# A new step table for the first stage, fixed for TensorE alone, with regrouped loads and plain v for four units

## The chip, the cores and the metric

The kernel runs on one core of a Trainium2 chip. The metric is device time in microseconds of one execution; the time before is 1538.48 us, the median of three runs (1537.49 to 1541.13).

## What is computed

Chunked attention over 8 batches, 8 heads, 576 positions and head size 64, in chunks of 64 positions, then two feed-forward layers on the 4608 tokens:

```python
scores = scale * np.matmul(q_c, k_c.transpose(0, 1, 2, 4, 3))
attn = np.exp(scores - max) ; attn = attn / (sum + 1e-09) ; x = np.matmul(attn, v_c)
x = (((x @ w1) * (x @ w2)) @ w3) @ w_out          # 512 -> 1024 -> 1024 -> 512
h = x @ w_in                                       # 512 -> 2048
out = (np.maximum(h, 0.0) + alpha * np.minimum(h, 0.0)) @ w_out2   # 2048 -> 512
```

The weights reach the kernel as 64-bit floats. It turns each into two 32-bit parts, a rounded high part (HI) and the rest (LO), and each product of the feed-forward layers is three TensorE passes over such parts.

## The kernel before

The tokens are nine blocks of 512 (`b`), each fed by two attention units of 256 tokens (`u = 2b, 2b + 1`). The whole program is written out at build time, and a scheduling layer adds all waits. It also chooses the order of each engine's instructions by a plan of its own, with the order in the code as priority; an instruction that is handed to `keep_in_program_order` keeps its place instead. In the kernel before, the switch `pinned` is off during the first stage, so all three compute engines are ordered by the plan there, and turned on for TensorE's matmuls and transposes after it.

The first stage is what this text is about. It does the attention of units 0 to 5, the first projections of blocks 0 to 2 (`LEAD`), the conversion of 40 weight halves, and the product of `w3` and `w_out` (the fold). Its steps stand in the string `STARTUP` (line 36), letter and number:

- An attention unit `n`: `S` scores (32 small matmuls on TensorE), `M` maximum (VectorE), `X` 16 exps (ScalarE), `Y` sum and division (VectorE), `T` 8 transposes (TensorE), `P` copy of these out of PSUM (ScalarE), `V` 32 small matmuls with v (TensorE), `c` copy of the HI part into `x` (ScalarE), `d` subtraction for the LO part (VectorE).
- A weight half `n`, of 40: `A` an Abs out of the loaded `raw` (ScalarE), `B` three operations (VectorE), `C` the HI cast (ScalarE), `D` two operations (VectorE), `E` two more (VectorE). Halves 0 to 15 are `w1` and `w2` (tiles `wa`), 16 to 23 `w_out` (`wo`), 24 to 39 `w3` (`w`). `raw` has three buffers, and step `A` issues the load of the half two further on; the `w3` halves share the three buffers of tag `gs`.
- A projection group: `a b.f` and `b b.f`, 12 matmuls of 512 columns each, with weight halves 2f and 2f + 1 (into banks `a` and `b`, or a pair `ab`, in turns); `k` copies the first out (ScalarE), `m` multiplies (VectorE) and writes the product to DRAM (`g_dram`).
- A fold: `h f.half`, 12 matmuls from `w3` half 24 + 2f + half and four `wo` halves; `s` and `w` split its sum into HI and LO (ScalarE, VectorE).

`lent` (line 396) says which PSUM pair a unit's scores take: units 0 and 2 `att`, 1 and 3 `p23`, all others `att`. A fold's sums lie in the two banks of `p23`, one pair for two values of f. All loads are issued by SP, one after the other (`load_unit`, line 214: q and k of a unit as two transfers, v as six, since half of v is written to the other half of the partitions, `1::2`, so that a unit's V goes round all four 64 x 64 quadrants of the array).

After the stage, `load_g` reads the products of blocks 0 to 2 back, `proj_wc` multiplies them by the folded weights (tiles `acc`), and units 6 and 7 are mixed in; then blocks 3 to 8 and the last layer follow, which the change leaves alone.

Of the kernel before, what the change touches and what calls it, by code (L numbers as in the profile page):

```python
# [34 lines left out]

STARTUP = """
    S0 M0 X0 A0 S1 Y0 M1 T0 P0 B0 X1 V0 D0 c0 Y1 C0 A1 d0 T1 A2 E0 P1 S2 B1 V1 A3 c1 M2 C1 d1 X2 D1 S3 B2 a0.0 M3 C2
    Y2 X3 E1 T2 D2 b0.0 B3 P2 Y3 k0.0 V2 C3 A4 m0.0 T3 c2 E2 P3 d2 a0.1 A5 D3 B4 V3 k0.1 E3 C4 c3 D4 b0.1 A6 d3 q4
    q5 E4 a1.0 m0.1 A7 B5 a0.2 k1.0 B6 C5 D5 C6 b1.0 D6 k0.2 E5 E6 A8 b0.2 m1.0 A9 B7 a1.1 m0.2 C7 D7 B8 a0.3 k1.1
    E7 C8 D8 A10 b1.1 k0.3 B9 E8 C9 b0.3 m1.1 A11 D9 B10 a1.2 m0.3 C10 E9 a0.4 k1.2 D10 A12 B11 b1.2 k0.4 E10 C11  # L40
    D11 A13 b0.4 m1.2 E11 B12 A14 a1.3 m0.4 C12 D12 a0.5 B13 k1.3 E12 C13 b1.3 D13 k0.5 A15 B14 E13 b0.5 C14 m1.3
    A16 D14 a1.4 m0.5 E14 B15 A17 a0.6 k1.4 B16 C15 D15 b1.4 C16 k0.6 D16 E15 b0.6 m1.4 A18 E16 B17 a1.5 A19 m0.6
    C17 D17 a0.7 k1.5 B18 E17 C18 b1.5 k0.7 D18 A20 B19 b0.7 m1.5 C19 E18 D19 A21 a1.6 m0.7 E19 S4 B20 k1.6 A22 b1.6
    M4 C20 D20 X4 B21 a1.7 m1.6 E20 b1.7 D21 k1.7 C21 Y4 A23 m1.7 T4 E21 P4 B22 A24 V4 B23 C22 c4 D22 C23 d4 E22 S5
    D23 A25 M5 E23 X5 B24 B25 D24 C24 C25 Y5 A26 E24 T5 P5 D25 h0.0 A27 B26 E25 C26 V5 D26 A28 h0.1 c5 B27 d5 C27 s0
    E26 a2.0 w0 A29 D27 h1.0 k2.0 B28 E27 C28 b2.0 D28 A30 B29 h1.1 m2.0 C29 E28 D29 A31 a2.1 s1 B30 w1 C30 E29 h2.0
    k2.1 D30 A32 B31 b2.1 E30 C31 D31 A33 h2.1 m2.1 E31 a2.2 s2 B32 A34 w2 C32 D32 h3.0 k2.2 B33 E32 C33 b2.2 D33
    A35 B34 h3.1 m2.2 C34 E33 D34 a2.3 A36 s3 B35 w3 C35 h4.0 E34 k2.3 D35 A37 b2.3 B36 E35 C36 h4.1 m2.3 A38 D36
    B37 a2.4 s4 E36 C37 w4 A39 h5.0 D37 k2.4 B38 E37 b2.4 C38 D38 B39 h5.1 m2.4 C39 E38 a2.5 s5 D39 w5 E39 h6.0 k2.5
    b2.5 h6.1 m2.5 a2.6 s6 w6 h7.0 k2.6 b2.6 h7.1 m2.6 a2.7 s7 w7 b2.7 k2.7 m2.7  # L50
# [8 lines left out]
def tile_attention_moe_moe(ctx: ExitStack, tc: tile.TileContext, qkv: bass.AP, w12: bass.AP,  # L59
# [30 lines left out]
    pinned = [False]  # L90

    def matmul(*args, **kw):
        ins = nc.tensor.matmul(*args, **kw)  # L93
        if pinned[0]:
            tc.keep_in_program_order(ins)

    def transpose(*args, **kw):
        ins = nc.tensor.transpose(*args, **kw)  # L98
        if pinned[0]:
            tc.keep_in_program_order(ins)  # L100

    def split(dst, src):

        nc.scalar.copy(dst[:, HI], src)  # L104
        nc.vector.tensor_tensor(out=dst[:, LO], in0=src, in1=dst[:, HI].bitcast(F32), op=ALU.subtract)  # L105
# [51 lines left out]
    def convert_b(i):
# [3 lines left out]
        nc.vector.tensor_scalar(out=m, in0=m, scalar1=EXP_MIN, scalar2=EXP_MAX, op0=ALU.max, op1=ALU.min)  # L161
        nc.vector.tensor_scalar(out=m.bitcast(U32), in0=m.bitcast(U32), scalar1=3, scalar2=0x3FFFFFF8,
                                op0=ALU.logical_shift_left, op1=ALU.bitwise_and)
        nc.vector.scalar_tensor_tensor(out=m.bitcast(U32), in0=conv_raw[i][:, :, 1], scalar=0xC0000000,  # L164
                                       in1=m.bitcast(U32), op0=ALU.bitwise_and, op1=ALU.bitwise_or)

    def convert_c(i):
        nc.scalar.copy(w_g[conv[i]][:, HI], conv_m[i])

    def convert_d(i):  # L170

        p = conv_p[i] = tmp("p")
# [31 lines left out]
    def mm3(ps, stat, mov, first, last):  # L204
        for i, (s, m) in enumerate(PASSES):
            matmul(ps, stat(s), mov(m), start=first and i == 0, stop=last and i == 2)
# [3 lines left out]

    x_t = {}
    un = {}

    def load_unit(u):
# [4 lines left out]
        else:  # L219
# [3 lines left out]
                 "e": granule(slots[3], "e", F32).rearrange("p j (a h k) -> p j a h k", a=4, h=2)}  # L223
        v = un[u]["v"]
# [342 lines left out]
```

## Time and profile before

| | us |
|---|---|
| median of three runs | 1538.48 |
| profiled execution | 1539.19 |
| its span | 1537.4 |
| TensorE busy in the span | 1494.1 (97%) |
| VectorE busy | 780.4 (51%) |
| ScalarE busy | 422.6 (27%) |
| share of TensorE in the chain that ended last | 89% |

The profile is of one execution. Its time is the span, from the first to the last instruction, and 1.8 us around it. Busy shares are means over stages: in the last four fifths of the span TensorE is busy 9 tenths or more of every slice, so what can be read for the first stage has to be read from its own stretch, here 0 to 245 us.

### The profile page before, as it was taken

To read this page: it belongs to the slowest core of one execution; us is meant where nothing else is said; L and a number is where in the kernel's file an instruction comes from. 1 tells how busy PE (TensorE), PEld (TensorE's weight loads), DVE (VectorE), ACT (ScalarE), POOL (GpSimd) and SP (SyncE) were. 2 spreads that over 40 slices of the span, in tenths; PEclk is the share of its full clock that TensorE was granted. 3 is DMA by queue.
4 is the path that set the end of the run, shared out by engine and by line. 5 is a ranking of instruction groups with operands and counts; after the bars stand their busy time and mean duration, and the time that the engine had idled before them with its cause. 6 is when DMAs were issued, how large, how long until landed. Compare 5 with 4: busy or idle time off the path is not lost.

```text
span 1537.4 us, 21112 instructions
## 1 busy us (share of the span) xinstructions
PE 1494.1 (97%) x8688; PEld 1231.1 (80%) x8688; DVE 780.4 (51%) x1250; ACT 422.6 (27%) x1107; POOL 0.7 (0%) x6
## 2 busy tenths in 40 slices
PE   4997999999999999999999999999999999999998
PEld 3785787788888888888888888888888888888887
DVE  4989963366667665331334344343434344343433
ACT  6535323444444443331211111111111111111111
POOL 0000000000000000000000000000000000000000
PEclk9998999999999999999999999999999999999999
DMA  8644425644545456236501000010101000000000
GB/s 249 190 165 151 136 98 165 192 153 155 188 163 192 151 179 206 83 103 199 165 0 55 1 20 36 1 55 0 56 0 38 18 7 35 1 28 0 28 1 28
DMA packets 65041, 141.89 MB, mean 92 GB/s; under 512 B 6833, under 2 KB 25265, under 8 KB 64945
## 3 DMA queue, kind: packets, MB, share of 16 engines
q1 hardware_dynamic: 64944, 140.54, 27.7%
q8 instruction: 68, 1.11, 0.3%
q14 instruction: 29, 0.23, 0.0%
HBM read 98.57 MB, written 41.94 MB: 91 GB/s over the span
## 4 chain that ended last, share of the span: by engine, by line
PE 89%; DVE 4%; DMA 3%; ACT 2%; SPq 1%; issue 1%; ACTq 0%; DVEq 0%
PE acc L93 38%; PE a L93 23%; PE b L93 22%; PE wc L93 2%; PE ab L93 2%; DMA v<-in_qkv 1%; ACT e L258 1%; PE sc L93 1%; PE pa L93 1%; DMA raw<-in_wo 1%; DMA raw<-in_w 1%; PE pa L98 1%; DVE p L175 1%; DMA g<-g_dram 1%; DVE m L164 0%
## 5 line engine op out<-in xcount | busy, mean ns | idle before, releaser
L93 PE MATMUL acc<-w,gs 128*128 128x512 f32 x1728 | 414.7, 389 | 0.0
L93 PEld LDWEIGHTS acc<-w,gs 128*128 128x128 f32 x1728 | 324.4, 188 | 67.2
L104 ACT CAST gs<-g 128x512 fp32r<-128x512 f32 x168 | 104.6, 622 | 660.7 <-DVE g L378 635.0
L93 PE MATMUL acc<-gs,wc 128*128 128x512 f32 x864 | 210.2, 395 | 3.8 <-DVE gs L105 3.8
L93 PE MATMUL a<-y,w 128*128 128x512 f32 x864 | 207.5, 389 | 0.0
L93 PE MATMUL b<-y,w 128*128 128x512 f32 x864 | 207.5, 389 | 0.0
L93 PEld LDWEIGHTS acc<-gs,wc 128*128 128x128 f32 x864 | 161.6, 189 | 40.4 <-DVE gs L105 5.5
L93 PEld LDWEIGHTS b<-y,w 128*128 128x128 f32 x864 | 162.2, 188 | 33.7
L93 PEld LDWEIGHTS a<-y,w 128*128 128x128 f32 x864 | 162.2, 188 | 33.7
L105 DVE TENSOR_TENSOR gs<-g,gs 128x512 fp32r<-128x512 f32 x168 | 116.2, 692 | 134.7 <-ACT gs L104 132.7
L93 PE MATMUL a<-x,wa 128*128 128x512 f32 x720 | 175.1, 393 | 2.4 <-DVE x L297 2.4
L93 PE MATMUL b<-x,wa 128*128 128x512 f32 x720 | 175.7, 393 | 0.0
L93 PEld LDWEIGHTS a<-x,wa 128*128 128x128 f32 x720 | 136.3, 190 | 31.3 <-DVE x L297 2.9
L93 PEld LDWEIGHTS b<-x,wa 128*128 128x128 f32 x720 | 133.5, 188 | 27.6
L377 DVE TENSOR_SCALAR g<-b,alpha_sb 128x512 f32<-128x512 f32 x72 | 54.0, 750 | 177.7 <-PE b L93 177.7
L377 DVE TENSOR_SCALAR g<-a,alpha_sb 128x512 f32<-128x512 f32 x72 | 54.0, 750 | 162.6 <-PE a L93 162.6
L258 ACT ACTIVATE e<-sc,mx 128x64 f32<-128x64 f32 x288 | 85.7, 348 | 31.4 <-DVE mx L247 31.4
L331 DVE TENSOR_TENSOR a<-b,a 128x512 f32<-128x512 f32 x60 | 41.3, 688 | 95.1 <-PE b L93 84.4
L258 ACT ACTIVATION_READ_ACCUMULATOR e<-sc,mx 128x1 f32 x288 | 69.7, 242 | 0.0
L93 PE MATMUL ab<-x,wa 128*128 128x512 f32 x288 | 69.3, 390 | 0.0
L486 ACT COPY a<-a 128x512 f32<-128x512 f32 x48 | 28.6, 596 | 131.2 <-PE a L93 112.5
L93 PEld LDWEIGHTS ab<-x,wa 128*128 128x128 f32 x288 | 53.9, 188 | 11.2
(56 smaller groups left out, 995.9 us busy)
## 6 DMA issues: line engine op xcount, KB each, us to landing
qk<-in_qkv SPq DMA_DIRECT2D x36, 512.0 KB, 4.9
raw<-in_w2nd SPq DMA_DIRECT2D x32, 512.0 KB, 4.0
w_dram<-wm SPq DMA_DIRECT2D x32, 512.0 KB, 3.3
w<-w_dram SPq DMA_DIRECT2D x32, 512.0 KB, 3.3
y_dram<-y SPq DMA_DIRECT2D x36, 256.0 KB, 2.9
yraw<-y_dram SPq DMA_DIRECT2D x18, 512.0 KB, 4.3
out<-o SPq DMA_DIRECT2D x36, 256.0 KB, 2.1
raw<-in_w SPq DMA_DIRECT2D x16, 512.0 KB, 4.2
```

The costliest lines, as they stand in the source:

```text
L93: ins = nc.tensor.matmul(*args, **kw)
L98: ins = nc.tensor.transpose(*args, **kw)
L104: nc.scalar.copy(dst[:, HI], src)
L105: nc.vector.tensor_tensor(out=dst[:, LO], in0=src, in1=dst[:, HI].bitcast(F32), op=ALU.subtract)
L175: nc.vector.scalar_tensor_tensor(out=p, in0=conv_raw[i][:, :, 0], scalar=2.0 ** -52, in1=p, op0=ALU.mult, op1=ALU.mult)
L258: nc.scalar.activation(out=e[:, j, a, h], in_=s[:, h2, n * D:(n + 1) * D], func=AF.Exp, bias=mx[:, h2, n:n + 1], scale=SCALE, accum_out=sm ...
L331: nc.vector.tensor_tensor(out=a, in0=ps, in1=a, op=ALU.mult)
L377: nc.vector.tensor_scalar(out=g, in0=ps, scalar1=0.0, scalar2=alpha_sb[:, f:f + 1], op0=ALU.min, op1=ALU.mult)
L486: nc.scalar.copy(a, pa)
```

## The change

The table `STARTUP` is new. Its order is now fixed for TensorE from the first instruction on, while ScalarE and VectorE still follow the plan, with the table as priority. `InOrder` wraps the three engines; its switch is on for TensorE alone. Units 4 and 5 stand earlier in the table, the folds stand later and in runs, and the last two steps, `g`, load the first two products back before the last fold's split. Here is one line of the old table and one of the new, of the stretch where units 4 and 5 stand:

```diff
-    M4 C20 D20 X4 B21 a1.7 m1.6 E20 b1.7 D21 k1.7 C21 Y4 A23 m1.7 T4 E21 P4 B22 A24 V4 B23 C22 c4 D22 C23 d4 E22 S5
+    b1.0 m0.3 k1.0 B9 A10 D9 C9 a0.4 m1.0 E9 A11 M4 b0.4 k0.4 B11 X4 D11 a1.1 m0.4 B10 b1.1 D10 C11 A12 E11 C10 k1.1
...
+    class InOrder:
+        def __init__(self, engine):
+            self.engine, self.on = engine, engine is nc.tensor
+        def __getattr__(self, name):
+            op = getattr(self.engine, name)
+            def call(*args, **kw):
+                ins = op(*args, **kw)
+                if self.on:
+                    tc.keep_in_program_order(ins)
+            return call
+    pe, act, dve = InOrder(nc.tensor), InOrder(nc.scalar), InOrder(nc.vector)
...
+    CROSS = 4
...
+    def load_v(u):
         v = un[u]["v"]
         for j in range(2):
-            nc.sync.dma_start(out=un[u]["qk"][j], in_=qkv[2 * u + j, :, 0:2])
-        for j in range(2):
+            if u < CROSS:
+                nc.sync.dma_start(out=v[:, j].rearrange("p a x -> p (a x)"), in_=qkv[2 * u + j, :, 2])
+                continue
...
-                            a, h = 2 * i + odd, h2 ^ odd
+                            a, h = 2 * i + odd, h2 ^ (odd if u >= CROSS else 0)
...
-            if f % 2 == 0:
-                ab["fold"] = pair("p23", "wc")
-        ps = ab["fold"][:, f % 2]
+            ab["fold", f] = pair(("att", "p23")[f % 2], "wc")[:, 0]
+        ps = ab["fold", f]
...
+    act.activation(out=work.tile([P, 1], F32, tag="warm", name="warm", bufs=1), in_=ident[:, 0:1], func=AF.Exp)
     for u in range(4):
-        load_unit(u)
-        if u < RAW:
-            convert_load(u)
+        unit_tiles(u)
+    for load, n in ((load_qk, 0), (convert_load, 0), (load_qk, 1), (load_v, 0), (convert_load, 1), (load_v, 1),
+                    (load_qk, 2), (convert_load, 2), (load_v, 2), (load_qk, 3), (load_v, 3)):
+        load(n)
     nc.sync.dma_start(out=alpha_sb, in_=alpha)
-    lent = {0: "att", 1: "p23", 2: "att", 3: "p23"}
+    steps = [(b, f) for b in range(LEAD) for f in range(NF1)]
+    lent = {1: "p23", 3: "p23", 5: "p23"}
...
+        elif kind == "g":
+            load_g(*steps[n])
...
-    pinned[0] = True
+    act.on = dve.on = False
     load_unit(2 * LEAD)
-    load_g(*steps[0])
-    load_g(*steps[1])
```

So for units 0 to 3 v is loaded as two plain transfers a unit instead of six, and their V alternates between two quadrants of the array; the exps of these units write their results in the plain order too. A one-column exp stands ahead of everything on ScalarE. Unit 5 uses the pair `p23`, and each fold takes one bank of `att` or of `p23` by turns.

SP issues the loads at the start of the program in this order before, here the first ones:

```order
L226 DMA qk<-in_qkv 128x1024 x2
L229 DMA v<-in_qkv 128x2x128
L230 DMA v<-in_qkv 64x2x128
L231 DMA v<-in_qkv 64x2x128
L229 DMA v<-in_qkv 128x2x128
L230 DMA v<-in_qkv 64x2x128
L231 DMA v<-in_qkv 64x2x128
L143 DMA raw<-in_w 128x1024
L226 DMA qk<-in_qkv 128x1024 x2
```

and in this order now:

```order
L238 DMA qk<-in_qkv 128x1024 x2
L148 DMA raw<-in_w 128x1024
L238 DMA qk<-in_qkv 128x1024 x2
L244 DMA v<-in_qkv 128x512 x2
L148 DMA raw<-in_w 128x1024
L244 DMA v<-in_qkv 128x512 x2
L238 DMA qk<-in_qkv 128x1024 x2
L148 DMA raw<-in_w 128x1024
```

The second pair of `qk` (unit 1) stands in the fourth place instead of the tenth, and v of a unit is one row of two.

TensorE's first instructions before, up to the first projection groups (`sc` scores, `pa<-ident,e` transposes, `pa<-pt,v` values, `a`, `b` and `ab` projections):

```order
L93 MATMUL sc<-qk 64x64 x64
L98 MATMUL pa<-ident,e 128x128 x8
L93 MATMUL pa<-pt,v 64x64 x32
L98 MATMUL pa<-ident,e 128x128 x8
L93 MATMUL sc<-qk 64x64 x32
L93 MATMUL pa<-pt,v 64x64 x32
L93 MATMUL sc<-qk 64x64 x32
L93 MATMUL a<-x,wa 128x512 x12
L93 MATMUL b<-x,wa 128x512 x6
```

and now:

```order
L100 MATMUL sc<-qk 64x64 x64
L100 MATMUL pa<-ident,e 128x128 x8
L100 MATMUL pa<-pt,v 64x64 x32
L100 MATMUL pa<-ident,e 128x128 x8
L100 MATMUL pa<-pt,v 64x64 x32
L100 MATMUL sc<-qk 64x64 x32
L100 MATMUL a<-x,wa 128x512 x12
L100 MATMUL b<-x,wa 128x512 x12
L100 MATMUL ab<-x,wa 128x512 x12
L100 MATMUL sc<-qk 64x64 x32
L100 MATMUL pa<-ident,e 128x128 x8
```

The scores of unit 3 moved from ahead of the first group to behind the third, and those of unit 2 behind the values of unit 1.

TensorE again, where the folds (`wc`) begin, before:

```order
L93 MATMUL ab<-x,wa 128x512 x24
L98 MATMUL pa<-ident,e 128x128 x8
L93 MATMUL pa<-pt,v 64x64 x32
L93 MATMUL sc<-qk 64x64 x32
L93 MATMUL wc<-wo,w_1485 128x512 x12
L98 MATMUL pa<-ident,e 128x128 x8
L93 MATMUL wc<-wo,w_1571 128x512 x4
L93 MATMUL pa<-pt,v 64x64 x32
L93 MATMUL wc<-wo,w_1571 128x512 x8
L93 MATMUL a<-x,wa 128x512 x12
L93 MATMUL wc<-wo,w_1612 128x512 x12
L93 MATMUL b<-x,wa 128x512 x12
```

and now:

```order
L100 MATMUL ab<-x,wa 128x512 x24
L100 MATMUL wc<-wo,w_1657 128x512 x12
L100 MATMUL wc<-wo,w_1686 128x512 x12
L100 MATMUL wc<-wo,w_1752 128x512 x12
L100 MATMUL wc<-wo,w_1795 128x512 x12
L100 MATMUL a<-x,wa 128x512 x12
L100 MATMUL b<-x,wa 128x512 x12
L100 MATMUL wc<-wo,w_1815 128x512 x12
L100 MATMUL wc<-wo,w_1826 128x512 x12
L100 MATMUL wc<-wo,w_1868 128x512 x12
```

The steps of units 4 and 5 are gone from this place (they stand among the groups of blocks 0 and 1), and the folds stand in runs of three to five where every one had a projection group behind it.

## Rows read from the trace of the kernel before

**Rows 1.** The page, chain that ended last: share by engine.

```profile
PE 89%; DVE 4%; DMA 3%; ACT 2%; SPq 1%; issue 1%; ACTq 0%; DVEq 0%
```

**Rows 2.** Stretches: length; busy (instructions) by engine; PE clock; DMA share, GB/s.

```profile
core 0: us, PE busy (x) PEld busy (x) DVE busy (x) ACT busy (x) POOL busy (x), PEclk, DMA share, GB/s
0.00:20.00 20.00, 6.91 (x152) 5.78 (x156) 6.57 (x12) 8.17 (x39) 0.70 (x6) 1.00 0.91 277
20.00:40.00 20.00, 11.23 (x266) 10.01 (x259) 13.79 (x26) 15.38 (x71) 0.00 (x0) 0.86 0.74 223
...
60.00:80.00 20.00, 20.00 (x90) 16.57 (x89) 18.94 (x38) 7.20 (x12) 0.00 (x0) 1.00 0.52 164
...
120.00:140.00 20.00, 16.35 (x191) 13.11 (x189) 18.75 (x37) 12.28 (x44) 0.00 (x0) 1.00 0.48 160
140.00:160.00 20.00, 12.71 (x160) 9.39 (x160) 19.46 (x39) 12.37 (x44) 0.00 (x0) 0.66 0.37 120
```

**Rows 3.** TensorE's timeline, 16 to 67: start, busy us, what, [idle before, releaser].

```profile
16.53 1.94 PE L98 MATMUL pa<-ident,e 128*128 128x128 f32 x8 [0.89 <-DVE e L265]
19.57 1.99 PE L93 MATMUL pa<-pt,v 64*64 64x64 f32 x64 [1.10 <-ACT pt L276]
...
35.65 1.99 PE L93 MATMUL sc<-qk 64*64 64x64 f32 x64 [4.18 <-DVE x L297]
37.57 4.74 PE L93 MATMUL a<-x,wa 128*128 128x512 f32 x12
...
47.68 1.16 PE L93 MATMUL pa<-pt,v 64*64 64x64 f32 x64
...
61.93 2.88 PE L93 MATMUL b<-x,wa 128*128 128x512 f32 x12
64.65 2.88 PE L93 MATMUL ab<-x,wa 128*128 128x512 f32 x12
```

**Rows 4.** Timeline of ScalarE and VectorE, 8 to 27.

```profile
8.50 1.28 ACT L258 ACT_TABLE_LOAD   x1 [8.50 <-DVE mx L247]
9.79 0.31 ACT L258 ACTIVATE e<-sc,mx 128x64 f32<-128x64 f32 x1
...
14.43 0.75 ACT L155 ACTIVATE m<-raw 128x512 f32<-128x512 f32 x1
...
18.50 1.01 ACT L276 COPY pt<-pa 128x1024 f32<-128x1024 f32 x1 [3.32 <-PE pa L98]
...
24.04 1.11 ACT L300 CAST x<-pa 128x1024 fp32r<-128x1024 f32 x1
...
24.93 0.74 ACT L168 CAST wa<-m 128x512 fp32r<-128x512 f32 x1
...
25.92 1.22 DVE L297 TENSOR_TENSOR x<-pa,x 128x1024 fp32r<-128x1024 f32 x1
```

**Rows 5.** Transfers, 0 to 40: bytes moved, in 40 slices of 1 us.

```profile
GB/s 0 57 246 377 391 324 171 166 266 303 401 396 332 225 255 272 262 418 387 291 229 277 271 311 397 379 306 157 104 229 295 336 422 234 0 0 16 0 258 242
```

**Rows 6.** TensorE's timeline around units 4 and 5, and at the stage's end.

```profile
135.95 1.06 PE L98 MATMUL pa<-ident,e 128*128 128x128 f32 x8 [1.82 <-DVE e L265]
...
142.54 1.98 PE L93 MATMUL sc<-qk 64*64 64x64 f32 x64 [3.21 <-DVE x L297]
...
149.97 4.39 PE L93 MATMUL wc<-wo,w 128*128 128x512 f32 x10 [3.02 <-DVE w L180]
...
161.01 3.02 PE L93 MATMUL a<-x,wa 128*128 128x512 f32 x12 [1.41 <-DVE x L297]
...
245.30 4.60 PE L93 MATMUL acc<-gs,wc 128*128 128x512 f32 x12 [2.39 <-DVE gs L105]
```

**Rows 7.** VectorE's timeline in its dense stretch; the last row ends conversion 7.

```profile
68.94 0.68 DVE L179 TENSOR_TENSOR m<-m,wa 128x512 f32<-128x512 f32 x1
69.54 0.42 DVE L161 TENSOR_SCALAR m<-m 128x512 f32<-128x512 f32 x1
69.88 0.69 DVE L180 TENSOR_TENSOR wa<-m,p 128x512 fp32r<-128x512 f32 x1
```

**Rows 8.** The timeline where conversion 39, the last of the stage, ends.

```profile
222.68 0.69 DVE L180 TENSOR_TENSOR w<-m,p 128x512 fp32r<-128x512 f32 x1
```

More of the change, by code (lines that the diff above doesn't have):

```diff
@@ L36 @@
 STARTUP = """
[L37 to L41, printed above, removed]
@@ L88, in tile_attention_moe_moe @@
     w2_dram = {(f, h): tc.dram_tile([P, 2, TB], F32, name=f"w2_dram{f}_{h}") for f in range(NF2) for h in range(2)}
[L90 to L100, printed above, removed]
+    class InOrder:
[9 more added lines that the diff above has]
+    pe, act, dve = InOrder(nc.tensor), InOrder(nc.scalar), InOrder(nc.vector)
     def split(dst, src):
-        nc.scalar.copy(dst[:, HI], src)
-        nc.vector.tensor_tensor(out=dst[:, LO], in0=src, in1=dst[:, HI].bitcast(F32), op=ALU.subtract)
+        act.copy(dst[:, HI], src)
+        dve.tensor_tensor(out=dst[:, LO], in0=src, in1=dst[:, HI].bitcast(F32), op=ALU.subtract)
     def tmp(name):
@@ L205, in mm3, with unit_tiles @@
         for i, (s, m) in enumerate(PASSES):
-            matmul(ps, stat(s), mov(m), start=first and i == 0, stop=last and i == 2)
+            pe.matmul(ps, stat(s), mov(m), start=first and i == 0, stop=last and i == 2)
+    CROSS = 4
     x_t = {}
     un = {}
-    def load_unit(u):
+    def unit_tiles(u):
         if u < 4:
@@ L223, in load_unit, with load_qk @@
                  "e": granule(slots[3], "e", F32).rearrange("p j (a h k) -> p j a h k", a=4, h=2)}
+    def load_unit(u):
+        unit_tiles(u)
+        load_qk(u)
+        load_v(u)
+    def load_qk(u):
+        for j in range(2):
+            nc.sync.dma_start(out=un[u]["qk"][j], in_=qkv[2 * u + j, :, 0:2])
+    def load_v(u):
         v = un[u]["v"]
         for j in range(2):
-            nc.sync.dma_start(out=un[u]["qk"][j], in_=qkv[2 * u + j, :, 0:2])
-        for j in range(2):
+            if u < CROSS:
+                nc.sync.dma_start(out=v[:, j].rearrange("p a x -> p (a x)"), in_=qkv[2 * u + j, :, 2])
+                continue
             vs = qkv[2 * u + j, :, 2].rearrange("p (a x) -> p a x", a=4)
@@ L296, in attn_out @@
         if lo:
-            nc.vector.tensor_tensor(out=xs[LO], in0=pa, in1=xs[HI].bitcast(F32), op=ALU.subtract)
+            dve.tensor_tensor(out=xs[LO], in0=pa, in1=xs[HI].bitcast(F32), op=ALU.subtract)
             un.pop(u)
         else:
-            nc.scalar.copy(xs[HI], pa)
+            act.copy(xs[HI], pa)
     wc_g = {}
@@ L318, in fold_split @@
             wc_g[f] = granule(24 + f, "wc")
-        dst, ps = wc_g[f], ab["fold"][:, f % 2]
+        dst, ps = wc_g[f], ab["fold", f]
         if lo:
-            nc.vector.tensor_tensor(out=dst[:, LO], in0=ps, in1=dst[:, HI].bitcast(F32), op=ALU.subtract)
+            dve.tensor_tensor(out=dst[:, LO], in0=ps, in1=dst[:, HI].bitcast(F32), op=ALU.subtract)
         else:
-            nc.scalar.copy(dst[:, HI], ps)
+            act.copy(dst[:, HI], ps)
     def proj1(b, f, which, ps):
@@ L330, in product @@
     def product(b, f, a, ps):
-        nc.vector.tensor_tensor(out=a, in0=ps, in1=a, op=ALU.mult)
+        dve.tensor_tensor(out=a, in0=ps, in1=a, op=ALU.mult)
         if b < LEAD:
@@ L376, in proj2 @@
         g = tmp("g2")
-        nc.vector.tensor_scalar(out=g, in0=ps, scalar1=0.0, scalar2=alpha_sb[:, f:f + 1], op0=ALU.min, op1=ALU.mult)
-        nc.vector.scalar_tensor_tensor(out=g, in0=ps, scalar=0.0, in1=g, op0=ALU.max, op1=ALU.add)
+        dve.tensor_scalar(out=g, in0=ps, scalar1=0.0, scalar2=alpha_sb[:, f:f + 1], op0=ALU.min, op1=ALU.mult)
+        dve.scalar_tensor_tensor(out=g, in0=ps, scalar=0.0, in1=g, op0=ALU.max, op1=ALU.add)
         split_g(b, (f, 2), g)
@@ L420, in tile_attention_moe_moe @@
             a = ab[tuple(rest)][2] = tmp("a")
-            nc.scalar.copy(a, ab[tuple(rest)][0])
+            act.copy(a, ab[tuple(rest)][0])
         elif kind == "b":
@@ L456, in unit_steps @@
         return [first, second, third, fourth]
-    pinned[0] = True
+    act.on = dve.on = False
     load_unit(2 * LEAD)
-    steps = [(b, f) for b in range(LEAD) for f in range(NF1)]
-    load_g(*steps[0])
-    load_g(*steps[1])
     todo = {}
@@ L485, in tile_attention_moe_moe @@
             a = tmp("a")
-            nc.scalar.copy(a, pa)
+            act.copy(a, pa)
             if parts and f % 4 == 0:
```

64 lines of the change are left out of this document (35 added, 29 removed).

## The prediction

> **What bounds the kernel now.** I read the page's chain first: TensorE carries 89% of it [rows 1], so time is won only where TensorE waits or runs slowly. The table of 20 us stretches says where that is [rows 2]: it is busy 6.91 and 11.23 us in the first two, full at 60 to 80, then 16.35 and 12.71 at 120 to 160, the last at a granted clock of 0.66 (1.0 is 2.4 GHz). All of that lies in the first stage, before the first acc matmul at 245.30. TensorE's timeline gives its parts [rows 3, 6]: the first full group of 12 matmuls starts at 37.57, groups follow at 2.72 us (61.93, 64.65), and from 37.57 to 245.30 there are 207.7 us. In them lie 64 groups (174.1), two S, four T and four V of the attention units (1.16, 1.06 and 1.16 each, 11.2) and 1.9 for the first group, run cold (4.74 against 2.88). The remaining 20.5 us are waits and half clock. The named waits are 1.82, 3.21, 3.02 and 1.41 around units 4 and 5, and 2.39 for the first g [rows 6]. VectorE sets the pace of what can be brought forward: 18.94 of 20 us busy at 60 to 80, 19.46 at 140 to 160 [rows 2].
>
> I write S, T, V for a unit's scores, transposes and values on TensorE, X for its exps, P and c for its two ScalarE copies, d for VectorE's subtraction, as the table of steps does.
>
> **The loads and unit 0 and 1: the start moves from 37.57 to 29.5.** Before, q and k of unit 1 are issued behind six v pieces and a weight half, some 3.0 MB with themselves; now they are 2.5 MB. The rate by single us is 377 and 391 GB/s while q and k of unit 0 move and 171 and 166 just after, when the v pieces are under way [rows 5]. The first four slices hold 1.07 MB, the other 1.4 take 4 to 5 us at 277 to 390 GB/s, so unit 1's scores can end at 11 to 12; before, they stood ahead of the transposes at 16.53 [rows 3]. X0 loses the table load of 1.28 at its head [rows 4], since the one-column exp loads the table while nothing is ready: 8.5 + 16 exps from 9.79 to 14.43 (4.64) gives 13.1. Then comes the Abs of the second weight half (0.75), which needs its load, 3.5 MB into the queue; then X1, to 18.5 (before, it ends where c0 starts, 24.04). On ScalarE stand behind it a weight cast (0.7) and P0 (1.01): 20.2. The rest is a chain of cold steps: V0 1.99, T1 1.94, P1 1.01, V1 1.99, c1 1.11, d1 1.22 [rows 3, 4], 9.3 us, so 29.5. S2 (1.99) lies beside c1 and d1. I take 29.5. Bounds: 26 (clock up from T1 on, loads never late) to 34 (X1 waits for its weight half until 17).
>
> *What the pages say of the loads.* The Trainium skill, DMA: Bandwidth & Descriptors, Specifications, puts line rate at pieces of 512 B and more; the v pieces have 512 B, so by it plain v saves issue time only. This trace does not agree: 166 to 171 GB/s against 377 to 391. By the page's rule the mean rate of 277 GB/s [rows 2] would stay, the second weight half would land near 14 and the start be about 30.5.
>
> **V of units 0 to 3, uncrossed.** The same 32 matmuls now alternate between two quadrants of the array where they went round four. The trace has only four-quadrant V: 1.16 us, 1.99 cold [rows 3]. The price is between a little below nothing and a doubling, 2 x 1.99 + 2 x 1.16 = 6.3 us in all. I take nothing: S visits its quadrants in another sequence and takes the same 1.99, which looks like a limit per matmul and not per quadrant.
>
> **The order on TensorE.** Units 4 and 5 now come among the groups of blocks 0 and 1, with groups between S, T and V; before, each of their steps waited for its neighbour. That takes away the 9.5 us of waits named above and the half clock around them. The first two g loads, their casts and subtractions move ahead of the last split (and on SP ahead of unit 6's loads), so the 2.39 goes, and the first acc group, cold at 4.60, should take 2.88: another 1.7. The last fold's split (ScalarE, VectorE) ends some 1.4 us after the last fold, while acc matmuls of the other bank pair run: 0.4 left. Unit 6 loads into slots that the last folds read, so its load now starts two groups before acc; two groups and the twelve acc matmuls, about 7.6 us, hide it, and what lands later is a wait at its scores.
>
> New waits. TensorE can't change its order any more, so it stands where a weight is late. VectorE's order has, up to and with the last operation of conversion 7 (needed by b0.3), 46 us of work at 0.60 for a two-operand instruction, 0.34 for TENSOR_SCALAR and 1.22 for 1024 columns [rows 4, 7]; before, it was 48 and done at 70.6, so 22 us were idle. If the idle time shrinks with the start by some 8, conversion 7 is done at 62. TensorE would like it at 29.5 + 1.9 + 7 x 2.72 + six unit steps (6.9) = 57. The loads of units 4 and 5, 3 MB in 16 issues, now stand on SP's queue between weight halves 5 and 9; at 277 GB/s they take 11 us, of which I count what these halves come late among the waits. So **5 us** of waits, bounds 0 to 9. After that TensorE has 56 groups and five unit steps, 158 us, and the last fold starts at 62 + 2.7 + 155 = 220; VectorE has 134 us of work to conversion 39. Before, 130 us of it took from 70.6 to 223.4 [rows 7, 8], 1.17 us for each; at that pace 39 is done at 62 + 157 = 219, just in time, and part of that pace was waiting for folds. But folds now run three to five in a row with only three w3 buffers, where before every fold had a projection group behind it. I take **3 us**, bounds 0 to 10.
>
> **The sum.** First acc at 29.5 + 174.1 + three S, four T, four V (12.4) + 1.9 + 5 + 3 + 0.4 = 226.3, against 245.30: 19.0. With 1.7 for the warm first acc group, 20.7 us. The rest of the kernel keeps its order. The profiled execution took 1539.2 (span 1537.4), 0.7 above the median; 1539.2 - 20.7 = 1518.5, and I say **1519**.
>
> **Rivals.** (1) *Conversions no earlier.* The early idle time of VectorE stays 22 us, because loads and ScalarE set it; conversion 7 at 70.6, 8.6 later: 1527. For: VectorE has little idle time left at 60 to 80 [rows 2]. Against: its idle 13 us of the first 20 [rows 2] come from the load order that changes. (2) *The loads bring nothing*, the first group starts at 37 since the engines that move data are the bound: 7.5 later, 1526. That is the case in which the change does not do what it says. For: data moves at 277 GB/s in the first 20 us [rows 2]. Against: 377 and 391 stand beside it where no v pieces move [rows 5]. (3) *V doubles*, two quadrants instead of four: +6.3, 1525. The mechanism is that matmuls of one quadrant follow each other without overlap; against it stands S. The Trainium skill, TensorEngine Tiling (Array Packing), Tiling Modes, has four independent tiles at 64 x 64, which would speak for it; no run here shows two. (4) *Slower: the runs of folds starve.* A w3 half is cast into a buffer that frees with the fold three before; the cast stands in ScalarE's queue, and behind it the next Abs and the copy that frees a projection bank. From the fourth fold on, 13 folds: if each exposes its cast (0.7), its two last VectorE operations (1.3) and a share of another conversion's, 2.8 us, that is 36 in place of my 3: 1552. It decides from 1.8 us a fold. Against: before, VectorE waited for such casts, but TensorE's timeline has no wait between the 1.41 at 161 and the 2.39 at 245 [rows 6], because groups lay between; now runs of 8 to 13 us are followed by 5 to 11 us of projections, in which the buffers refill.
>
> **How the numbers follow.** My case 57%; rival 1 14%, rival 3 10%, rival 2 8%, rival 4 7%, and 4% that losses of several kinds add up to no change. A measurement here tells 0.2% (3 us) from none. Faster: 57 + 14 + 10 + 8 = 89%; same 4%; slower 7%. My own case goes from 1509 (start at 27, no new waits from late weights) to 1528; rivals 1 to 3 lie at 1525 to 1527 with a few us of spread. The range 1509 to 1531 leaves out rival 4, the unchanged case and the ends of the rest, some 19%.
>
> **What would show it.** Right: first group of 12 at 27 to 32; X1 beginning within a us of X0's end; no TensorE wait over 1 us between 75 and 200; clock 1.00 at 140 to 160; first acc at 222 to 230 with a first group under 3 us. Wrong: the first group at 35 or later (loads); VectorE idle over 18 us before conversion 7 (rival 1); V at 2 us warm (rival 3); waits for w from VectorE or ScalarE before most folds (rival 4); long waits of unit 6's scores for q and k.

## The result: 15 us slower, since every 512-column matmul became slower

The changed kernel takes 1554.29 us (median of four runs, 1554.05 to 1554.65) against 1538.85 for the kernel before beside it: ratio 1.0099, 95% interval 1.0082 to 1.0117. The forecast was 1519, range 1509 to 1531. Spans of the profiled executions: 1552.4 after, 1537.4 before.

The first stage came out almost as forecast, though not term by term (see the part on why). The stretches of the profile after, the same ones as [rows 2]: length; busy us and instructions of TensorE, its weight loads, VectorE, ScalarE, GpSimd; granted clock; DMA share and GB/s.

```profile
0.00:20.00 20.00, 6.52 (x138) 5.39 (x138) 11.11 (x20) 13.55 (x71) 0.70 (x6) 1.00 0.92 343
20.00:40.00 20.00, 17.41 (x301) 14.98 (x302) 17.42 (x32) 13.18 (x45) 0.00 (x0) 1.00 0.76 260
60.00:80.00 20.00, 19.72 (x84) 15.39 (x83) 18.94 (x38) 11.61 (x44) 0.00 (x0) 1.00 0.51 159
120.00:140.00 20.00, 20.00 (x88) 16.05 (x87) 15.66 (x28) 7.81 (x13) 0.00 (x0) 1.00 0.39 131
140.00:160.00 20.00, 20.00 (x87) 16.09 (x86) 16.75 (x33) 7.10 (x13) 0.00 (x0) 1.00 0.46 154
```

The holes of [rows 2] are gone: TensorE is full from 120 to 160 where it had 16.35 and 12.71, and the clock there is 1.00 where it was 0.66. But look at the matmuls: in a full stretch there are 87 and 88 of them in 20 us, and the full stretch of before, 60 to 80, had 90. TensorE's timeline after (start, busy us, what, idle before and releaser) shows it group by group:

```profile
19.95 3.64 PE L100 MATMUL pa<-pt,v 64*64 64x64 f32 x64 [2.90 <-ACT pt L100]
...
30.23 3.06 PE L100 MATMUL a<-x,wa 128*128 128x512 f32 x12 [1.44 <-DVE x L100]
33.12 2.96 PE L100 MATMUL b<-x,wa 128*128 128x512 f32 x12
35.92 2.95 PE L100 MATMUL ab<-x,wa 128*128 128x512 f32 x12
...
43.74 2.08 PE L100 MATMUL pa<-pt,v 64*64 64x64 f32 x64
...
108.37 1.16 PE L100 MATMUL pa<-pt,v 64*64 64x64 f32 x64
...
225.83 3.23 PE L100 MATMUL acc<-gs,wc 128*128 128x512 f32 x12
...
1004.59 2.96 PE L100 MATMUL a<-y,w 128*128 128x512 f32 x12
1007.38 2.96 PE L100 MATMUL acc<-w,gs 128*128 128x512 f32 x12
```

Against [rows 3] and [rows 6] the first group starts 7.3 us earlier (30.23 for 37.57) and the first acc group 19.5 earlier (225.83 for 245.30). But the groups follow each other at 2.80 us (1004.59 to 1007.38; 33.12 to 35.92), where [rows 3] has 2.72. The timeline of before at the same place in the last stage, which the change leaves alone:

```profile
1005.12 2.88 PE L93 MATMUL a<-y,w 128*128 128x512 f32 x12
1007.84 2.88 PE L93 MATMUL acc<-w,gs 128*128 128x512 f32 x12
```

So a matmul of 512 columns went, in the mean of a group, from 226.7 ns (2.72 / 12) to 233.3, 6.67 ns more, at a granted clock of 1.00 in both (400 to 1500). There are 6240 such matmuls: 41.6 us. From the first acc to the end the kernel before takes 1537.4 - 245.30 = 1292.1 us, the one after 1552.4 - 225.83 = 1326.6: 34.5 lost there, 19.5 gained ahead of it, 15.0 in all. The pages say the same (busy us of TensorE and its weight loads, first of the page before, then of the page after, there with the chain that ended last):

```profile
PE 1494.1 (97%) x8688; PEld 1231.1 (80%) x8688; DVE 780.4 (51%) x1250; ACT 422.6 (27%) x1107; POOL 0.7 (0%) x6
```

```profile
PE 1528.3 (98%) x8688; PEld 1226.8 (79%) x8688; DVE 781.9 (50%) x1250; ACT 421.3 (27%) x1108; POOL 0.7 (0%) x6
...
PE 93%; DVE 3%; ACT 2%; DMA 1%; issue 0%; SPq 0%; ACTq 0%; DVEq 0%
```

TensorE is busy 34 us more with the same 8688 instructions; the weight loads are not longer.

### The profile page after: what moved, and what is told of

It is laid out like the page before. It is cut to its first block, busy times and chain, and to the rows that moved or that the text cites. A ratio compares the mean times of both kernels' runs of the same rounds, so it can differ in the third digit from the quotient of the medians.

```text
span 1552.4 us, 21097 instructions
## 1 busy us (share of the span) xinstructions
PE 1528.3 (98%) x8688; PEld 1226.8 (79%) x8688; DVE 781.9 (50%) x1250; ACT 421.3 (27%) x1108; POOL 0.7 (0%) x6
## 4 chain that ended last, share of the span: by engine, by line
PE 93%; DVE 3%; ACT 2%; DMA 1%; issue 0%; SPq 0%; ACTq 0%; DVEq 0%
PE acc L100 38%; PE b L100 23%; PE a L100 23%; PE ab L100 3%; PE wc L100 3%; PE pa L100 2%; ACT e L100 1%; DVE m L100 1%; PE sc L100 1%; DMA g<-g_dram 1%; DVE p L100 0%; DMA raw<-in_w 0%; DVE wa L100 0%; DVE e L100 0%; DVE mx L100 0%
## 5 line engine op out<-in xcount | busy, mean ns | idle before, releaser
L100 PE MATMUL acc<-w,gs 128*128 128x512 f32 x1728 | 426.6, 396 | 0.0
L100 PE MATMUL acc<-gs,wc 128*128 128x512 f32 x864 | 213.8, 398 | 2.2 <-DVE gs L100 2.2
L100 PE MATMUL b<-y,w 128*128 128x512 f32 x864 | 213.0, 395 | 0.0
L100 PE MATMUL a<-y,w 128*128 128x512 f32 x864 | 213.0, 395 | 0.0
L100 PE MATMUL b<-x,wa 128*128 128x512 f32 x720 | 179.7, 398 | 0.0
L100 DVE TENSOR_SCALAR m<-m 128x512 uint32<-128x512 uint32 (+1 forms) x144 | 59.8, 423 | 66.6 <-ACT m L100 65.8
L100 ACT COPY a<-a 128x512 f32<-128x512 f32 x60 | 35.9, 599 | 153.3 <-PE a L100 134.6
```

What stands on the lines that cost most here:

```text
L100: ins = op(*args, **kw)
```

## Experiments

What could slow all matmuls by 3%, in stages that kept their order? The build's addresses gave a suspect. The one-column exp writes a tile of its own, `warm`, of 32 bytes a partition. It is the first tile of the work pool, so `x`, `y`, `gs` and the `w3` halves (which share the `gs` buffers) all lie 32 bytes higher than before, while the weight granules (the tiles of the pool `gran`, which stands ahead of it) stay: `x` at byte 181216 instead of 181184, `gs` at 213984 instead of 213952, the first `wa` at 82624 in both. Rivals: TensorE's fixed order or its wrapper slows the stream; the folds' new PSUM banks; later, the exp itself.

### The tile taken away, made larger, and given to the kernel before

`e3_no_warm` drops the exp with its tile:

```diff
-    act.activation(out=work.tile([P, 1], F32, tag="warm", name="warm", bufs=1), in_=ident[:, 0:1], func=AF.Exp)
```

> The changed kernel without the one-column exp, so also without its tile. Theory: 2.72 us groups; the table load of 1.28 us comes back, either ahead of the first Abs where nothing waits for it (then 1514, as the 64-byte tile) or on unit 0's chain (then 1515). Rivals A and B: 1554 to 1556.

Measured: 1515.92 us (1515.5 to 1516.48), ratio 0.9854, interval 0.9839 to 0.9869. Groups follow at 2.72 us:

```profile
1003.17 2.88 PE L100 MATMUL a<-y,w 128*128 128x512 f32 x12
1005.89 2.88 PE L100 MATMUL acc<-w,gs 128*128 128x512 f32 x12
```

The order, the wrapper and the PSUM banks are the same as after, so those two rivals fall. It beats both kernels, and the one line costs 38.4 us.

`e2_before_shift32` gives the kernel before the same line, ahead of its first loads:

```diff
+    nc.scalar.activation(out=work.tile([P, 1], F32, tag="warm", name="warm", bufs=1), in_=ident[:, 0:1], func=AF.Exp)
```

> The kernel before with nothing added but a one-column exp into a 32-byte tile allocated first in the work pool. Theory: groups of 12 matmuls take 2.80 us in place of 2.72 everywhere, time 1538.9 + 6240 x 6.67 ns = about 1577 to 1580. Rivals A and B: 1538, less up to 1.3 for the table load that moves ahead.

Measured: 1578.41 (1577.05 to 1579.32), ratio 1.0257 (1.024 to 1.0274), as expected. Groups at 2.80:

```profile
1004.51 2.96 PE L93 MATMUL acc<-w,gs 128*128 128x512 f32 x12
1007.32 2.96 PE L93 MATMUL a<-y,w 128*128 128x512 f32 x12
```

`e1_warm64` makes the tile 64 bytes (`[P, 16]` for `[P, 1]`), since before all these tiles had begun at multiples of 64:

> The changed kernel with the one-column exp's tile 16 columns wide instead of one, so it takes 64 bytes a partition instead of 32; every instruction stands in the same place on its engine. Theory: every 512-column matmul went from 226.7 to 233.3 ns because that 32-byte tile moved x, gs and all other work tiles from addresses that are multiples of 64 bytes to odd multiples of 32; then groups of 12 take 2.72 us again, the first acc comes near 221, and the time is about 1514 (1554.3 less 6240 x 6.67 ns = 41.6, plus a little waiting for weights). Rival A (the order fixed from the first instruction on, through the wrapper, makes TensorE's stream slower): 2.80 us groups and 1554 as in the changed kernel. Rival B (the folds' banks in PSUM): 1554.

Measured: 1541.42 (1537.92 to 1543.1), ratio 1.0015 (1.0006 to 1.0025). A miss: projections and acc<-gs,wc ran at 2.75 to 2.76 us a group, folds and the last layer at 2.77 to 2.80. Alignment to 64 bytes is not the rule.

`e4_gs_shift32` adds to that a 32-byte tile ahead of `gs` (x 64 bytes and gs 96 above their old places), allocated when the first such buffer is:

```diff
+        if not padded:
+            padded.append(work.tile([P, 1], F32, tag="pad", name="pad", bufs=1))
+            act.activation(out=padded[0], in_=ident[:, 0:1], func=AF.Exp)
```

> The 64-byte tile at the head, and a second 32-byte tile just ahead of gs, so only the three gs buffers lie at odd multiples of 32 bytes. gs streams through the array (moving) in acc<-gs,wc; it is the loaded side (stationary) in acc<-w,gs and in the folds; x and y, moving in the projections, are aligned. If the moving side alone costs: acc<-gs,wc at 2.80 us a group and all others at 2.72, time about 1514 + 864 x 6.67 ns = 1520. If the stationary side costs too: the folds and acc<-w,gs at 2.80 as well, 1514 + 2784 x 6.67 ns = 1533. Rivals A and B: as the changed kernel, 1554.

Measured: 1549.08 (one run), groups of all kinds at 2.75 to 2.81. It could not tell the operands apart, as the 64 bytes beneath cost something themselves.

### The exp or its tile?

So far the exp and the shift had come together. `e6_warm128` (`[P, 32]`, exp kept):

> The changed kernel with the one-column exp kept and its tile made 128 bytes: work tiles 128 bytes higher than without it. Theory A (place repeats every 128 bytes, and a one-column exp is worth nothing): groups at 2.72 us in every kind, first group at 30.4, 1514 to 1518, as without the exp. Theory B (any move of the work tiles against the granules costs, 64 bytes half of it): groups at 2.75 to 2.80, 1540 to 1555. Theory C (it repeats, and the table load that the exp takes out of the first softmax is worth its 1.3 us): 1513 to 1515.

Measured: 1551.47 (1550.97 to 1551.72), groups at 2.80: theory B, and a reason to suspect the exp. Three runs separate them. `e9_exp_elsewhere` keeps the exp and puts its tile behind all others:

```diff
+    late = ctx.enter_context(tc.tile_pool(name="late", bufs=1))
-    act.activation(out=work.tile([P, 1], F32, tag="warm", name="warm", bufs=1), in_=ident[:, 0:1], func=AF.Exp)
+    act.activation(out=late.tile([P, 1], F32, name="warm"), in_=ident[:, 0:1], func=AF.Exp)
```

> The changed kernel with its one-column exp kept, but its output in a tile behind all others, so that no tile lies elsewhere than without it. Theory A (the tile's 32 bytes, which push the work tiles, slow the matmuls): groups of 12 at 2.72 us, 1514 to 1518. Theory B (the exp itself, an instruction more on ScalarE, slows them; so far exp and shift always came together): groups at 2.80 us, 1548 to 1556.

`e10_pad32_no_exp` and `e11_pad128_no_exp` have the tile and no exp:

```diff
-    act.activation(out=work.tile([P, 1], F32, tag="warm", name="warm", bufs=1), in_=ident[:, 0:1], func=AF.Exp)
+    nc.vector.memset(work.tile([P, 1], F32, tag="pad", name="pad", bufs=1), 0.0)    # [P, 32] in e11
```

> The changed kernel with the exp replaced by a VectorE memset of the same 32-byte tile: places as in the changed kernel, no exp. Theory A (place): groups at 2.80 us in every kind, 1551 to 1556. Theory B (the exp): groups at 2.72 us, 1514 to 1518.

> As the run before, with a 128-byte tile: work tiles 128 bytes above where they lie without it, no exp. Theory A (place, not repeating at 128 bytes): groups near 2.79 us, 1548 to 1553, as with the exp. Theory B (the exp): groups at 2.72 us, 1514 to 1518.

Measured: 1516.14 with the exp and no shift; 1554.23 and 1550.57 with the shift and no exp. It is the place, and the exp costs nothing. It brings nothing either. ScalarE's timeline after shows why: the table load stands at 0.73 and is done long before the first weight half lands, and the exp ran at 8.29, behind an Abs.

```profile
0.73 1.28 ACT L100 ACT_TABLE_LOAD   x1 [0.73 <-PEq L578]
7.73 0.66 ACT L100 ACTIVATE m<-raw 128x512 f32<-128x512 f32 x1 [5.72 <-DMA raw<-in_w]
8.29 0.19 ACT L100 ACTIVATE warm<-ident 128x1 f32<-128x1 f32 x1
```

Without the exp the table load stands at 0.73 just the same (`e3_no_warm`): with the regrouped loads an Abs comes first on ScalarE, and the table no longer waits for the first maximum as in [rows 4]. With the old issue order of the loads (`e12_old_loads`, below) the exps come first again and it waits. The table loads of these two:

```profile
0.73 1.28 ACT L100 ACT_TABLE_LOAD   x1 [0.73 <-PEq L577]
```

```profile
8.37 1.28 ACT L100 ACT_TABLE_LOAD   x1 [8.37 <-DVE mx L100]
```

### Which place?

`e5_all32` puts the 32 bytes into the constants, ahead of the weight granules too, so that all move together:

```diff
     alpha_sb = const.tile([P, NF2], F32, name="alpha_sb")
+    pad = const.tile([P, 1], F32, name="pad")
+    nc.vector.memset(pad, 0.0)
```

> The changed kernel without its one-column exp, with a 32-byte tile in the constants instead (one VectorE memset of it): weight granules and work tiles alike lie 32 bytes higher, so their distance to each other is as without the tile. Theory A (what counts is where moving and stationary data lie against each other): groups of 12 at 2.72 us, 1514 to 1518. Theory B (what counts is the address of each by itself): groups at 2.80 us in every kind, 1550 to 1556, since all operands now have the remainder 96 by 128 that the work tiles had in the changed kernel.

Measured: 1515.78, groups at 2.72. The distance between work tiles and weights counts, not the address.

`e13_gs_only32` moves `gs` and the `w3` halves alone, by a 32-byte tile just ahead of them, in the kernel without the exp:

> The changed kernel without the one-column exp, and a 32-byte tile (one memset) just before the three gs buffers: gs and the w3 halves, which share the buffers, lie 32 bytes higher, x, y, weights and all else where the fast kernels have them. Theory A (a matmul is slow when its own two operands lie badly against each other): acc<-gs,wc, acc<-w,gs and the folds at 2.80 us a group, a<-x,wa and a<-y,w at 2.72; 6.67 ns for 1728 + 1728 + 192 matmuls and those of the last stage that read gs, 20 to 25 us: 1535 to 1541. Theory B (any part of the work pool moved slows all): all at 2.80, 1550 to 1555. Theory C (only the moving operand's place counts): acc<-gs,wc slow, folds and acc<-w,gs fast: 1526 to 1529.

Measured: 1536.01 (1535.31 to 1538.93), and the groups by kind tell it inside one kernel. The columns are: busy us, mean ns of one matmul (its own length, some 160 ns longer than the step to the next). First `e13_gs_only32`:

```profile
L100 PE MATMUL acc<-w,gs 128*128 128x512 f32 x1728 | 425.4, 395 | 0.0
L100 PE MATMUL acc<-gs,wc 128*128 128x512 f32 x864 | 213.7, 398 | 1.8 <-DVE gs L100 1.8
L100 PE MATMUL a<-y,w 128*128 128x512 f32 x864 | 208.4, 390 | 0.0
...
L100 PE MATMUL b<-x,wa 128*128 128x512 f32 x720 | 175.4, 392 | 0.0
...
L100 PE MATMUL wc<-wo,w 128*128 128x512 f32 x192 | 45.6, 395 | 0.0
```

and `e3_no_warm`:

```profile
L100 PE MATMUL acc<-w,gs 128*128 128x512 f32 x1728 | 414.7, 389 | 0.0
L100 PE MATMUL acc<-gs,wc 128*128 128x512 f32 x864 | 208.8, 392 | 2.0 <-DVE gs L100 1.9
L100 PE MATMUL a<-y,w 128*128 128x512 f32 x864 | 207.5, 389 | 0.0
...
L100 PE MATMUL b<-x,wa 128*128 128x512 f32 x720 | 175.4, 392 | 0.0
...
L100 PE MATMUL wc<-wo,w 128*128 128x512 f32 x192 | 44.3, 389 | 0.0
```

The three kinds that read a shifted tile lose 6 ns each: `acc<-gs,wc`, where it streams (the moving operand), and `acc<-w,gs` and the folds `wc<-wo,w`, where it is the stationary operand, the one that a weight load brings into the array. The kinds that read `x` or `y`, whose groups alternate with these, lose 2 ns at most. So only matmuls at or beside a shifted tile are slow, whichever of the two operands it is: theory A against B and C.

Theory A says "its own two operands", and that is not quite what the trace shows. Here are groups of the last stage in `e13_gs_only32`, matmuls and, between the dots, the weight loads of the second group:

```profile
1004.46 2.90 PE L100 MATMUL a<-y,w 128*128 128x512 f32 x12
...
1006.96 2.75 PEld L100 LDWEIGHTS acc<-w,gs 128*128 128x128 f32 x12
...
1007.19 2.96 PE L100 MATMUL acc<-w,gs 128*128 128x512 f32 x12
1009.99 2.90 PE L100 MATMUL b<-y,w 128*128 128x512 f32 x12
```

Taken one by one, the matmuls of an `a<-y,w` or `b<-y,w` group start 226.7 ns apart from the second to the last (the first step, 231, may be the tail of the group ahead), but from the last one to the first of `acc<-w,gs` it is 235 (234 to 235 in all 141 such places of the last stage; 226 to 227 in `e3_no_warm`). That last matmul reads nothing shifted; what happens beside it is the load of the first `gs` weights, at 1006.96. So the next matmul's weights count too, against the columns that stream meanwhile. By the pitch that is 6.67 ns x 2784 = 18.6 us; measured 20.1, with the little that the groups of x and y lose. (The 25 in the expectation counted acc<-gs,wc twice.)

`e14_pad256` makes the pad 256 bytes; `e15_minus256` takes 256 bytes away from below `x` and `gs` by moving the small tiles of maxima and sums into a pool behind, in the kernel of `e7_swapped_heads` (below):

> As the run with 128 bytes, with 256: work tiles 256 bytes above their place without it. Theory A (place repeats every 256 bytes: x and gs lie at a multiple of 4096 plus 256 from the weights in the fast kernels): 2.72 us, 1514 to 1518. Theory B (it repeats later, or only that distance is good): 2.75 to 2.80, 1535 to 1556.

> The kernel with odd head pairs swapped, and the small tiles of maxima and sums put behind all others: x, y, gs and w3 halves lie 256 bytes lower, at a multiple of 4096 from the weights. Theory A (256 bytes are a period): 2.72 us, 1513 to 1515. Theory B (only the old distance is good): 2.75 to 2.80, 1530 to 1552. Theory C (a multiple of 4096 is better still than 256 beside it): below 2.72, down to 2.56 (512 columns at 2.4 GHz): under 1510.

Measured: 1516.17, and 1514.19 against 1514.15 for that kernel without the move; 2.72 us in both. Here is what the runs say together, the shift being against the kernel before, where `x` and `gs` lie a multiple of 4096 plus 256 bytes above the weights:

| shift of x and y, of gs and w3 (bytes) | us a group | kernel and time |
|---|---|---|
| 0, 0 | 2.72 | before 1538.85; without the exp 1515.92; exp elsewhere 1516.14 |
| all tiles +32, weights too | 2.72 | 1515.78 |
| +256, +256 | 2.72 | 1516.17 |
| -256, -256 | 2.72 | 1514.19 (swapped heads) |
| +32, +32 | 2.80 | after 1554.29; no exp 1554.23; before with it 1578.41 |
| +64, +64 | 2.75 to 2.80 | 1541.42 |
| +64, +96 | 2.75 to 2.81 | 1549.08 (one run) |
| +128, +128 | 2.79 to 2.80 | 1551.47; no exp 1550.57 |
| 0, +32 | 2.72 to 2.75 for x and y, about 2.80 for the rest | 1536.01 |

### What the other parts are worth

All of these have the tiles in their old places. `e12_old_loads` issues the first loads unit by unit as before, v still plain; `e8_crossed_v` loads all v crossed in six pieces as before (`CROSS = 0`), in the new issue order; `e16_order_only` does both, so that the new order is left, with its fixing on TensorE and its PSUM banks:

```diff
     for u in range(4):
-        unit_tiles(u)
-    for load, n in ((load_qk, 0), (convert_load, 0), (load_qk, 1), (load_v, 0), (convert_load, 1), (load_v, 1),
-                    (load_qk, 2), (convert_load, 2), (load_v, 2), (load_qk, 3), (load_v, 3)):
-        load(n)
+        load_unit(u)
+        if u < RAW:
+            convert_load(u)
```

> The changed kernel without the one-column exp and with the first loads issued as in the kernel before, unit by unit with a weight half behind each (v stays plain): the price of regrouping alone. Theory A (units 0 and 1 are what the first group waits for): q and k of unit 1 land 2 to 4 us later, first group at 32 to 35 instead of 30.4, total 1518 to 1521. Theory B (the regrouping brings nothing, plain v and the order did it): first group within 0.7 of 30.4, 1515 to 1517.

> The changed kernel without the one-column exp, with v of units 0 to 3 loaded crossed, in six pieces a unit, as in the kernel before; all else as it is. The V of four quadrants gives 4.4 us back. Theory A (the pieces move at 166 to 171 GB/s where the rest moves at 377 to 391, 1.75 us more a unit): first group 1 to 3 later than with plain v, total 1513 to 1518, no clear gain or loss. Theory B (pieces cost nothing that shows): first group 1 to 2.5 earlier, 1510 to 1513. Theory C (the pieces delay the weight halves too): waits for weights from VectorE before 62 us, over 1519.

> The changed kernel without the one-column exp, with the loads of the kernel before (its issue order, and v crossed in six pieces for all units): only the new order of the steps is left, and every tile lies as in the kernel before. Theory A (the order alone carries most of the gain, and loads and plain v add what they took when undone one by one, 2.1 and 2.4 us): 1519.5 to 1522. Theory B (their losses meet at the start of TensorE's first group and count once or hide behind later waits): 1518 to 1519.5. Theory C (the order needs the early loads): first group at 36 or later and 1523 to 1530.

Measured: 1518.05, 1518.30 and 1520.10 us (ratio of the last to the kernel before 0.9884, interval 0.9867 to 0.99). First groups, in this order:

```profile
34.47 4.60 PE L100 MATMUL a<-x,wa 128*128 128x512 f32 x12 [1.86 <-DVE x L100]
```

```profile
30.89 3.04 PE L100 MATMUL a<-x,wa 128*128 128x512 f32 x12 [0.84 <-DVE x L100]
```

```profile
34.80 3.04 PE L100 MATMUL a<-x,wa 128*128 128x512 f32 x12 [0.97 <-DVE x L100]
```

The order is worth some 18 us (no run has the new table without the fixing, or the fixing without the table), regrouping 2.1 and plain v 2.4; together these two are worth 4.2, so they nearly add. The 2.1 include the table load, which in `e12_old_loads` waits for the first maximum again. Crossed v brings the first group only 0.5 us later than the 30.36 without the exp, less than theory A's 1 to 3; most of its loss comes behind, where waits of 2.10 for unit 2's e and 0.84 for a late weight half appear, and a saving of 0.9 us a V does not pay for them (granted clock over 40 to 60: 0.91). The time fell between theories A and C. In the same order of steps and loads, the first 20 us move 266 GB/s with v crossed and 345 with v plain (`e3_no_warm`); no run separates the short rows of the pieces from the half of the partitions that four of the six write.

`e7_swapped_heads` keeps v plain and gets the four quadrants back in another way: the odd head pairs write to the other half of the partitions, and the host lays the rows of `w1` and `w2` of the odd 128-row tiles out in that order:

```diff
-                            a, h = 2 * i + odd, h2 ^ (odd if u >= CROSS else 0)
+                            a, h = 2 * i + odd, h2 ^ odd
...
+        w = w.reshape(k // 256, 2, 2, 64, f)
+        return np.stack([w[:, 0], w[:, 1, ::-1]], axis=1).reshape(k, f)
```

> The changed kernel without the one-column exp; all v is loaded plain, and the odd head pairs' outputs are written to the other half of the partitions, so the V matmuls go round four quadrants again; rows of w1 and w2 of the odd 128-row tiles are stored in the same order by the host's layout. Theory A (V's doubling is two quadrants against four): V at 1.16 us warm and about 2 cold, where the kernel without the exp has 2.08 and 3.68; with 1.7 of the cold ones' and 2 x 0.9 of the warm ones' and some 0.9 of unit 1's, 4.4 us: first acc at 218, 1510 to 1513. Theory B (the doubling comes from plain v's rows, not from the quadrants): V at 2.08, 1514 to 1518. Theory C (V is hidden by what units 0 and 1 wait for anyway): V at 1.16, but first acc later than 220 and 1513 to 1516.

Measured: 1514.15 (1513.69 to 1514.34), ratio 0.9846 (0.9828 to 0.9863), the fastest version here. First acc at 221.57 against 222.46. V is what theory A says, the total is theory C's:

```profile
20.08 1.98 PE L100 MATMUL pa<-pt,v 64*64 64x64 f32 x64 [2.90 <-ACT pt L100]
21.99 1.97 PE L100 MATMUL pa<-ident,e 128*128 128x128 f32 x8
...
42.95 1.16 PE L100 MATMUL pa<-pt,v 64*64 64x64 f32 x64
...
49.01 1.40 PE L100 MATMUL pa<-ident,e 128*128 128x128 f32 x8 [1.94 <-DVE e L100]
50.34 1.99 PE L100 MATMUL sc<-qk 64*64 64x64 f32 x64
```

and `e3_no_warm`:

```profile
19.92 3.68 PE L100 MATMUL pa<-pt,v 64*64 64x64 f32 x64 [2.90 <-ACT pt L100]
23.53 1.21 PE L100 MATMUL pa<-ident,e 128*128 128x128 f32 x8
...
49.87 1.06 PE L100 MATMUL pa<-ident,e 128*128 128x128 f32 x8 [1.00 <-DVE e L100]
50.91 1.16 PE L100 MATMUL sc<-qk 64*64 64x64 f32 x64
```

What V gains is given back next door: the transposes behind the first V take 1.97 instead of 1.21, TensorE waits 1.94 instead of 1.00 for unit 3's e, and the scores behind that take 1.99 instead of 1.16 (granted clock over 40 to 60: 0.91, in `e3_no_warm` 1.00). Of 4.4 us some 1.8 are left.

## Why the prediction was wrong, step by step

**The step that failed** is the sentence "The rest of the kernel keeps its order", with the 2.72 us of a group carried over as if it were a property of the instruction. The order was kept, the pace was not: the sum's 64 groups at 174.1 and all that follows rest on it. I had counted the one-column exp only as taking the table load off ScalarE's chain and did not ask what its output tile pushes. That term was missing altogether: 38.4 us, of which 35.4 lie behind the first acc (1326.6 against 1291.2 without the exp; 5472 matmuls x 6.67 = 36.5) and the rest ahead of it. None of the four rivals held it, and the one on the slower side had another mechanism (starving folds) that did not come about: between 62 and the first acc no TensorE wait over 0.15 us stands in the timeline after, and at the old pace, in `e3_no_warm`, none at a fold. That its 1552 lies near the measured 1554 is chance.

With the tiles in their old places the same order gives 1515.92, 3 us below the forecast and inside its range. So the terms can be checked one by one there, with these lines of `e3_no_warm`:

```profile
30.36 3.01 PE L100 MATMUL a<-x,wa 128*128 128x512 f32 x12 [1.44 <-DVE x L100]
...
60.67 2.57 PE L100 MATMUL ab<-x,wa 128*128 128x512 f32 x10 [0.38 <-DVE wa L100]
...
222.46 3.23 PE L100 MATMUL acc<-gs,wc 128*128 128x512 f32 x12
```

"Cold" is my word for the early steps that take nearly double their later time. In `e3_no_warm` the granted clock is 1.00 from 15 to 24 too, so it is not shown that the clock makes them long.

- **Start, 29.5:** 30.36 (30.23 after). The loads behaved as said: 343 GB/s in the first 20 us for 277 in [rows 2]. (The 1.07 MB of "the first four slices" are those of the first five; the time hardly changes.) X1 begins as X0 ends, one Abs between. The table load did leave X0's head, but not by the exp. Behind P0 errors cancel in part: V0 took 3.68 for 1.99, T1 behind it 1.21 for 1.94.
- **V at nothing:** wrong. Rival 3 was right that V nearly doubles, 3.64 cold and 2.08 warm for 1.99 and 1.16 in [rows 3], but not on its 6.3 us: taking the doubling away in `e7_swapped_heads` saves 1.8. The step that failed is the inference from S: that S takes as long in another sequence of the quadrants says nothing of two quadrants. The Trainium skill, TensorEngine Tiling (Array Packing), Tiling Modes, lists four tiles for 64 x 64, and its Key Properties there call tiles independent; 1.16 us with four in use and 2.08 with two agree with it.
- **Waits for units 4 and 5, and half clock:** gone, as said; 20.00 of 20 us at clock 1.00 from 120 to 160.
- **New waits, 5 and 3 us, and 1.9 for a cold first group:** too many. Unit 3's e costs 1.00; VectorE ends conversion 7 at 60.6 (forecast 62), TensorE waits 0.38 for it, and later 0.31 and 0.62; the folds wait for nothing. The first group is not cold: 3.01, where 4.74 stood in [rows 3]. From the first group to the first acc 192.1 us pass without the exp, where the sum has 196.8 (226.3 - 29.5). That outweighs the error on V.
- **Tail:** the 2.39 before the first acc is gone, and its first group takes 3.23 for 4.60 (forecast 2.88).
- **First acc, 226.3:** 225.83 looks like a hit, but that is luck: two errors cancel. At the old pace it is 222.46; the slow matmuls fill 3.4 us more.

Ahead of the run the list of the build's addresses would have shown that the change moves these tiles, which the order doesn't show. That such a move costs, no row of the kernel before could show: all its groups run at one placement.

## What to carry to other kernels

A pace read from a trace belongs to the places of the operands as well as to the instruction: when a change adds, drops or resizes any tile, however small, compare where the large operands lie, and put small tiles behind the large ones or pad them to 256 bytes; either kept the pace here. When a kernel gets slower after an edit of the start, look at the step between like matmuls in a stage that the edit leaves alone, before looking at waits. An operation that is cheaper by itself is worth only what its neighbours leave over.

## What the runs showed of the hardware

- A matmul of 512 columns with fp32r operands (the type of the HI and LO parts) starts 226.7 ns after the one before when stationary and moving tile lie a multiple of 256 bytes apart (three such distances of the tiles tried: 0, 256 and 512 over a multiple of 4096; the slices that a matmul reads begin at multiples of 512 bytes inside them), and, in the mean of a group, 229 to 234 ns after it when one is off by 32, 64, 96 or 128 bytes (96 in one run). Other offsets were not tried.
- The mechanism is open. That the distance counts points to two operands being read at the same time, and the 235 ns beside the first `gs` load of `e13_gs_only32` point to the next weights, loaded while the current columns stream. But that alone does not fit every step: in the kernel after, the step behind the last `acc<-w,gs` matmul of a group takes 235 to 236 ns, though the columns that stream and the next weights are both unmoved there, and only its own weights lie shifted. The Trainium skill, TensorE: Matmul & The Clock Gate, Step-by-step: what each phase is for, gives TensorE two independent read ports, one for either operand; by that the distance should not matter, and here it did.
- 64 x 64 matmuls that alternate between two quadrants take 2.08 us for the matmuls of one V, round four quadrants 1.16: the kernel after has both, at 43.74 and, for units 4 and 5 with crossed v, at 108.37 and 112.64, at a granted clock of 1.00 (40 to 60 and 100 to 116). With plain v and four quadrants (`e7_swapped_heads`) it is 1.16 as well, so it is the quadrants and not the way v is loaded.
